# Gated attention with memory and two feed-forward blocks on one core: first-half scores in fp32 from two heads' data in the row halves, mask on TensorE, memory products in row halves

## The chip, the cores and the metric

One core of one Trainium2 chip runs the whole program. The metric is device time in microseconds (us) of one execution; the lower the better. Three executions of the kernel before took 965.35, 965.72 and 968.41 us.

## What is computed

The input has 4 batches (B), 8 heads (H), 576 positions (S) and 64 values per head (D). For each head:

```python
scores = q @ k.T / sqrt(64); causal mask; a = softmax(scores); local = a @ v
q_p = phi(q)                      # phi(x) = where(x > 0, x, exp(x) - 1) + 1
mem = (q_p @ M_prev) / (q_p @ z_prev + 1e-6)
out = g * mem + (1 - g) * local   # g = sigmoid(beta), one number per head
```

The heads of a token side by side are 512 values; the 2304 tokens then go through two feed-forward blocks: `((x @ w1) * (x @ w2)) @ w3 @ w_out` (512 to 1024 to 1024 to 512) and `h = x @ w_in; (h * tanh(softplus(h))) @ w_out` (512 to 2048 to 512). Inputs and output are fp32.

## The kernel before

**Precision.** TensorE multiplies in two ways here. A product of two fp32 tiles is one call in the code and two pairs of weight load and matmul in the trace. Where a faster product is wanted, each operand is split into a rounded part (type fp32r, a cast on ScalarE, ACT) and a remainder (a subtraction on VectorE, DVE, `lo`, line 341 with `sub`, line 333), and two or three fp32r products are added in PSUM.

**Tasks.** A task is a pair of heads (128 partitions: 64 rows of one head, 64 of the other) of one batch. Batch 0 is split by queries: tasks 0 to 3 take positions 0 to 287 (`hfs == (0,)`, the "first halves"), tasks 4 to 7 positions 288 to 575; the tasks of batches 1 to 3 take all 576. Tasks 0 to 11 (`T.f32`, `AVF=12`) multiply values and memory in fp32, the later ones in fp32r.

**One head of a first half** goes through these steps. `load_qk` (465) brings K transposed and Q transposed into a tile `ld`, each twice, in the upper and the lower 64 partitions (128 x 672). `prep` (473) makes from it a tile `QK`: a cast on ACT of all 672 columns (480), the remainder of K in the lower half on DVE (484, 64x384) and the remainder of Q (485, 128x288). With K and its remainder stacked in the 128 rows, two fp32r products per piece give the scores: `SC` (530) issues for each of three pieces (288, 160 and 32 queries wide) two pairs of weight load and matmul into one PSUM bank. Then DVE adds the causal mask to the bank (560): one operation of 128x256 and one of 128x32. The maximum over keys is taken on ACT, DVE and GpSimd (571, 569, 580), `SE` (582) subtracts it and takes the exponential, and `AV` (604) multiplies by the values.

**Once per task**, `phi` (488) loads Q of both heads again into a tile `pl` and makes phi(Q) (`PH`); `MEM` (503) multiplies it by the memory, for each half of 288 queries: `fm`, one fp32 product with the block-diagonal 128x128 matrix of both heads, and `fn`, one with the two columns of z. Two copies on ACT move the results out: 128x288 into `mnl` (526) and 2x288 into rows 0 and 1 of `R` (528). `AV` of the second head ends the task: the norms in `R` go through DRAM and come back spread over the partitions (644 to 661), two DVE operations combine (662, 663), and the result becomes `x`, the input of the feed-forward part.

**Weights.** The feed-forward weights come as pairs of 32-bit words and are converted on the core (`conv`, 673: one operation on ACT, two on DVE; `load_w` adds a cast and a remainder). w3 and w_out of the first block are multiplied with each other first, in 64 fp32 products of 512 columns (`w3_mm`, 718, tiles `wB` and `wD`). This is what TensorE does between the heads of the first halves.

**The order.** Nothing is ordered by the chip's queues at run time alone: every step is recorded as an operation with an engine and a cost (`op`, 82), and `Recorder.schedule` (111) works out, before the program is built, in which order each engine gets them. TensorE takes the operation with the lowest recorded number, feed-forward work counting 300 more (`GB=300`), so attention goes first where it is ready; the other engines take the one with the longest tail behind it. All transfers are on the one queue of SyncE (SP), in that order. Tiles come from rows of buffers (`ld` and `QK` two each, `PH`, `M`, `R` and `pl` one, eight PSUM banks `g`); an operation that needs a buffer waits until all users of its former owner are done. A changed cost therefore changes the order of the whole list.

The second feed-forward block runs after all attention is done, from about 580 us on.

Of the kernel before, what the change touches and what calls it, by code (L numbers as in the profile page):

```python
# [10 lines left out]
BF16 = mybir.dt.bfloat16  # L11
I32 = mybir.dt.int32
AF = mybir.ActivationFunctionType
# [249 lines left out]
def kernel(  # L263
    ctx: ExitStack,
    tc: tile.TileContext,
    qk: bass.AP,
    q: bass.AP,
    v: bass.AP,
    mz: bass.AP,
    beta: bass.AP,  # L270
    moe_w1: bass.AP,
# [76 lines left out]

    mask = const.tile([P, P], BF16, name="mask")
    eps = const.tile([P, 1], F32, name="eps")  # L350
    bt = const.tile([P, NP], F32, name="bt")
# [14 lines left out]

    fb, fg, fm_ = Fixed(bt), Fixed(gsc), Fixed(mask)
    fx2 = [Fixed(x2d) for _ in range(2 * B)]
# [6 lines left out]
    def triangle():  # L375
        idx, low = tri.tile[:, 0], tri.tile[:, 1]
        nc.vector.memset(mask, 0.0)
        for y in range(1, 4):
            nc.vector.memset(mask[32 * y:32 * y + 32, 0:32 * y], NEG)
        nc.vector.memset(idx[:, 0:1], 0.0)  # L380
        for y in range(5):
            nc.vector.tensor_scalar(out=idx[:, 1 << y:2 << y], in0=idx[:, 0:1 << y], scalar1=float(1 << y), scalar2=None, op0=ALU.add)
        nc.vector.transpose(low, idx)
        nc.vector.tensor_tensor(out=low, in0=idx, in1=low, op=ALU.is_lt)
        for y in range(4):
            r = slice(32 * y, 32 * y + 32)
            nc.vector.tensor_scalar(out=mask[r, r], in0=low[r], scalar1=NEG, scalar2=None, op0=ALU.mult)

    op("dve", 1300, triangle, w=[tri, fm_])

# [50 lines left out]
    def load_vm(T):  # L441
        j = T.nj
        n = 2 * j * DV
        if T.f32:
            M = T.M = buf("M", [P, VZ])
            dma(lambda: Vf.tile[:, T.i % 2, 0:j], lambda: v[T.b, T.p, :, 0:j], 512 * n, w=[(Vf, T.i % 2)])
            dma(lambda: M.tile, lambda: mz[T.b, T.p], 66560, w=[M])
            return
        raw = buf("vr", [P, VZ + 2 * NJ * DV])
        mr = lambda: raw.tile[:, 0:VZ]  # L450
        vr = lambda: raw.tile[:, VZ:VZ + n].rearrange("p (j t d) -> p j t d", t=2, d=DV)
        dma(vr, lambda: v[T.b, T.p, :, 0:j], 512 * n, w=[(raw, 0)])
        dma(mr, lambda: mz[T.b, T.p], 66560, w=[(raw, 1)])

        M = T.M = buf("M", [P, 2 * VZ], F32R)
        act(VZ, lambda: M.tile[:, 0:VZ], mr, [(raw, 1)], [(M, 0)])
        for a, b, c in ((0, P, VZ + 2), (P, VZ, VZ)):
            lo(b - a, lambda a=a, b=b, c=c: M.tile[:, c:c + b - a], lambda a=a, b=b: mr()[:, a:b], lambda a=a, b=b: M.tile[:, a:b], [(raw, 1), (M, 0)], [(M, 1)])
        act(n, lambda: Vb.tile[:, 0, 0:j], vr, [(raw, 0)], [(Vb, 0)])
        lo(n, lambda: Vb.tile[:, 1, 0:j], vr, lambda: Vb.tile[:, 0, 0:j], [(raw, 0), (Vb, 0)], [(Vb, 1)])  # L460

    def load_qk(T, t):
        h = 2 * T.p + t
        T.qk = getattr(T, "qk", {})
        d = T.qk[t] = buf("ld", [P, KQ])
        q0 = SK + T.x0
        for y, (a, b) in enumerate({(0,): [(K3, SK + HS)], (1,): [(0, SK), (SK + HS, KQ)], (0, 1): [(0, KQ)]}[T.hfs]):  # L470
            dma(lambda a=a, b=b: d.tile[:, a:b], lambda a=a, b=b: qk[T.b, h, :, a:b], 512 * (b - a), w=[(d, y)])

    def prep(T, t):
        d = T.qk[t]
        T.Q = getattr(T, "Q", {})
# [12 lines left out]
    def phi(T):  # L488
# [5 lines left out]
        ev = lambda: e.tile[:, 0:w]  # L494
        dma(xv, lambda: q[T.b, 2 * T.p:2 * T.p + 2, :, T.x0:T.x0 + w].rearrange("t d s -> (t d) s"), 512 * w, w=[x1])
        act(w, ev, xv, [x1], [e], False, AF.Exp)
        act(w, xv, xv, [x1], [x1], False, AF.Identity, bias=one)
        op("dve", t_dve(w), lambda: nc.vector.scalar_tensor_tensor(out=ev(), in0=ev(), scalar=1.0, in1=xv(), op0=ALU.min, op1=ALU.max), r=[e, x1], w=[e])
# [4 lines left out]
    def MEM(T):  # L503
# [3 lines left out]
        for hf in T.hfs:  # L507
            pm, pn = gbuf(), gbuf()
            qs = T.qs(HS * hf, HS * hf + HS)
            if T.f32:  # L510
                rd, cost, nz = [PH, M], 2 * 248, 2
                fm = lambda pm=pm, qs=qs: mm(pm.tile[:, 0:HS], M.tile[:, 0:P], PH.tile[:, qs], True, True)
                fn = lambda pn=pn, qs=qs: mm(pn.tile[0:2, 0:HS], M.tile[:, P:VZ], PH.tile[:, qs], True, True)
            else:
                rd, cost, nz = [(z, y) for z in (PH, M) for y in range(2)], 3 * t_mm(HS), 4

                def fm(pm=pm, qs=qs):
                    for y, (a, b) in enumerate(HL):
                        mm(pm.tile[:, 0:HS], M.tile[:, (VZ + 2) * a:(VZ + 2) * a + P], PH.tile[:, b, qs], y == 0, y == 2)

                def fn(pn=pn, qs=qs):
                    mm(pn.tile[0:4, 0:HS], M.tile[:, P:VZ + 2], PH.tile[:, 0, qs], True, False)
                    mm(pn.tile[0:4, 0:HS], M.tile[:, P:VZ + 2], PH.tile[:, 1, qs], False, True)

# [5 lines left out]
    def SC(T, t):  # L530
        Q = T.Q[t]
        T.m = m = buf("t", [P, T.w])
        T.s = []
        mkey = []
        for i, pieces in enumerate(T.banks):
            s = gbuf()
            T.s.append(s)

            def f(s=s, pieces=pieces):
                for j, q0, q1, c in pieces:  # L540
                    o = s.tile[:, c:c + q1 - q0]
                    kc = (j * P + K3) % SK
                    for y in range(2):
                        qc = SK + y * S + q0
                        mm(o, Q.tile[:, kc:kc + P], Q.tile[:, qc:qc + q1 - q0], y == 0, y == 1)

            op("pe", sum(2 * t_mm(q1 - q0) for _, q0, q1, _ in pieces), f, r=[(Q, x) for x in T.qkeys], w=[s])
            for i2, cs, m0, m1 in T.masks:
                if i2 != i:
                    continue  # L550
# [53 lines left out]
    def AV(T, t):  # L604
# [38 lines left out]
        rb = buf("Rr", [P, 2, W])  # L643
        dma(lambda: d0.tile[0:2], lambda: R.tile[0:2, :], 9216, r=[(R, (2, hf)) for hf in T.hfs], w=[(d0, 0)])
        dma(lambda: d0.tile[2:4], lambda: R.tile[32:65:32, :], 9216, r=[(R, (x, z)) for x in range(2) for z in range(len(T.outs))], w=[(d0, 1)])
# [349 lines left out]

_INS = ['qk', 'q', 'v', 'mz', 'beta', 'moe_w1', 'moe_w2', 'moe_w3', 'moe_w_out', 'moe2_w_in', 'moe2_w_out']
_OUTS = [((2304, 512), 'float32')]
# [49 lines left out]
```

## Time and profile before

| | |
|---|---|
| median of three executions | 965.72 us (965.35 to 968.41) |
| the profiled execution | 965.84 us |
| its span, first to last instruction | 964.1 us |
| TensorE (PE) busy | 945.7 us, 98% |
| VectorE (DVE) busy | 725.8 us, 75% |
| ScalarE (ACT) busy | 607.0 us, 63% |
| GpSimd (POOL) busy | 86.4 us, 9% |

"PE" is matmuls and "PEld" weight loads, which overlap them. Matmuls are pipelined: one that is shown as 0.6 us long may follow the one before it after 0.4 us, so the distance between two starts is the better measure of what a matmul costs, and a PE that is 98% busy isn't at its peak for all that time. The granted clock of TensorE is 1.00 in all slices of the span.

### The profile page before, as it was taken

What the parts mean: (1) busy time and instruction counts of PE and PEld (TensorE: products, weight loads), DVE (VectorE), ACT (ScalarE), POOL (GpSimd) and SP (SyncE); (2) the same over time, 40 slices, a digit from 0 to 9 for tenths busy, and PEclk for the clock granted to TensorE, in tenths of its full rate; (3) what the DMA queues carried; (4) which work ended last, traced back from release to release, by engine and by line L of the source; (5) the groups of instructions that cost most, each with busy time, mean ns of one, the idle gap of its engine ahead of it and who ended that gap; (6) DMA issues with size and microseconds to landing.
All of it is one profiled execution on the core that took longest, in us unless ns stands there. A gap on an engine that the chain in (4) does not pass through costs nothing.

```text
span 964.1 us, 15222 instructions
## 1 busy us (share of the span) xinstructions
PE 945.7 (98%) x5440; PEld 808.9 (84%) x5440; DVE 725.8 (75%) x1643; ACT 607.0 (63%) x1240; POOL 86.4 (9%) x70
## 2 busy tenths in 40 slices
PE   6999999999999999999999999999999999999998
PEld 3454878778999999999999988888888888998997
DVE  7999999899999989896653987547554756565663
ACT  6677877778797778775433776446444544554653
POOL 1210012322222012120000000000000000000000
PEclk9999999999999999999999999999999999999999
DMA  9689655542433422302641740020002001100000
GB/s 351 215 246 303 201 167 153 156 141 82 142 98 91 151 75 83 107 26 83 203 153 49 228 167 1 1 81 7 1 1 83 1 0 32 46 1 17 34 1 33
DMA packets 48316, 96.62 MB, mean 100 GB/s; under 512 B 11024, under 2 KB 23344, under 8 KB 48240
## 3 DMA queue, kind: packets, MB, share of 16 engines
q1 hardware_dynamic: 48240, 95.64, 31.3%
q8 instruction: 43, 0.70, 0.3%
q14 instruction: 33, 0.27, 0.1%
HBM read 85.85 MB, written 9.77 MB: 99 GB/s over the span
## 4 chain that ended last, share of the span: by engine, by line
PE 67%; DVE 18%; ACT 6%; DMA 4%; issue 3%; SPq 1%; POOL 0%; DVEq 0%; ACTq 0%; POOLq 0%
PE g L330 67%; DVE t L347 4%; DVE QK L333 3%; DMA Rr<-d 2%; DVE e L333 1%; DVE e L347 1%; ACT t L339 1%; DVE mnl L347 1%; DVE g L560 1%; SPq L327 1%; DVE u L333 1%; DVE t L686 1%; ACT mnl L337 1%; DMA wA<-in_moe_w_out_dram 1%; ACT R L337 1%
## 5 line engine op out<-in xcount | busy, mean ns | idle before, releaser
L330 PE MATMUL g<-u,wA 128*128 128x288 f32 (+2 forms) x1008 | 162.6, 314 | 1.0 <-ACT u L337 0.6
L330 PEld LDWEIGHTS g<-u,wA 128*128 128x128 f32 x1008 | 147.2, 188 | 9.9 <-ACT u L337 1.0
L347 DVE TENSOR_TENSOR t<-g,t 128x288 f32<-128x288 f32 (+6 forms) x344 | 121.3, 380 | 22.2 <-PE g L330 14.4
L580 POOL PARTITION_ALL_REDUCE t<-t x64 | 85.8, 1342 | 352.0 <-DVE t L347 282.5
L330 PE MATMUL g<-x,wB 128*128 128x288 f32 x768 | 110.7, 298 | 0.8 <-DVE t L347 0.8
L330 PEld LDWEIGHTS g<-x,wB 128*128 128x128 f32 x768 | 104.7, 188 | 3.3 <-DVE t L347 1.4
L339 ACT ACTIVATE x<-x,two 128x512 f32<-128x512 f32 (+1 forms) x80 | 54.4, 680 | 70.8 <-DVE x L830 70.8
L339 ACT ACTIVATE x<-g 128x512 f32<-128x512 f32 (+1 forms) x98 | 55.0, 561 | 65.2 <-PE g L330 63.9
L330 PE MATMUL g<-e,V 128*65 128x320 f32 (+12 forms) x576 | 90.3, 303 | 1.9 <-ACT e L339 1.5
L833 DVE SCALAR_TENSOR_TENSOR x<-g,x 128x512 f32<-128x512 f32 (+1 forms) x80 | 51.0, 637 | 43.0 <-ACT x L339 42.6
L330 PEld LDWEIGHTS g<-e,V 128*65 128x65 f32 (+1 forms) x576 | 66.2, 136 | 20.3 <-ACT e L339 3.0
L829 DVE TENSOR_SCALAR x<-x 128x512 f32<-128x512 f32 (+1 forms) x80 | 31.8, 397 | 61.8 <-ACT x L339 60.0
L330 PE MATMUL g<-QK 128*128 128x320 f32 (+7 forms) x464 | 72.8, 298 | 5.2 <-DVE QK L333 5.1
L337 ACT CAST x<-x 128x512 fp32r<-128x512 f32 (+1 forms) x80 | 46.1, 577 | 50.4 <-DVE x L347 50.3
L330 PEld LDWEIGHTS g<-QK 128*128 128x128 f32 x464 | 64.0, 193 | 14.8 <-DVE QK L333 7.8
L333 DVE TENSOR_TENSOR t<-x 128x512 fp32r<-128x512 f32 (+1 forms) x80 | 50.9, 637 | 31.9 <-ACT x L337 30.6
L330 PE MATMUL g<-wB,wD 128*128 128x512 f32 x128 | 61.6, 619 | 3.9 <-DVE wD L686 2.1
L333 DVE TENSOR_TENSOR QK<-ld,QK 64x640 fp32r<-64x640 f32 (+1 forms) x80 | 61.7, 772 | 3.5 <-ACT QK L337 1.9
L330 PE MATMUL g<-x,wD 128*128 128x288 f32 x384 | 57.0, 298 | 0.0
L337 ACT COPY t<-g 128x288 f32<-128x288 f32 (+2 forms) x96 | 36.5, 394 | 32.5 <-PE g L330 24.7
L330 PE MATMUL g<-x,wE 128*128 128x288 f32 x384 | 56.2, 300 | 0.5 <-DVE e L347 0.4
L347 DVE TENSOR_TENSOR x<-x 128x512 f32<-128x512 f32 (+1 forms) x80 | 51.0, 637 | 6.0
(147 smaller groups left out, 1815.6 us busy)
## 6 DMA issues: line engine op xcount, KB each, us to landing
ld<-in_qk_dram SPq DMA_DIRECT2D x24, 608.0 KB
u<-in_moe_w_dram SPq DMA_DIRECT2D x26, 512.0 KB
Rr<-d SPq DMA_DIRECT2D x24, 288.0 KB
mnl<-in_moe_w_out_dram SPq DMA_DIRECT2D x11, 512.0 KB
mnl<-in_moe_w_in_dram SPq DMA_DIRECT2D x11, 512.0 KB
x2d<-t SPq DMA_DIRECT2D x16, 288.0 KB
out_dram<-x SPq DMA_DIRECT2D x18, 256.0 KB
wA<-in_moe_w_out_dram SPq DMA_DIRECT2D x8, 512.0 KB
```

Source lines behind the costliest of these rows:

```text
L327: op("sp", max(500, nbytes / 340.0), lambda: nc.sync.dma_start(out=dst(), in_=src()), r, w)
L330: nc.tensor.matmul(out=o, lhsT=lhsT, rhs=rhs, start=start, stop=stop)
L333: eng.tensor_tensor(out=o, in0=a, in1=b, op=ALU.subtract)
L337: op("act", t_act(n, psum), lambda: nc.scalar.copy(out=o(), in_=i()), r, w)
L339: op("act", t_act(n, psum), lambda: nc.scalar.activation(out=o(), in_=i(), func=func, **kw), r, w)
L347: op(eng, t_dve(n) if eng == "dve" else t_pool(n), lambda: e.tensor_tensor(out=o(), in0=a(), in1=b(), op=alu), r, w)
L560: nc.vector.tensor_tensor(out=o, in0=o, in1=mv, op=ALU.add)
L580: op("pool", 430 + 2.6 * (b - a), lambda mv=mv: nc.gpsimd.partition_all_reduce(mv(), mv(), P, bass_isa.ReduceOp.max), r=[(m, x)], w=[(m, x)])
L686: op("dve", t_dve(512), lambda: nc.vector.scalar_tensor_tensor(out=ci(), in0=ci(), scalar=3, in1=lw(), op0=ALU.logical_shift_left, op1=ALU ...
L829: op("dve", t_dve(n, True), lambda: nc.vector.tensor_scalar(out=w_(), in0=u(), scalar1=E20, scalar2=2.0, op0=ALU.min, op1=ALU.add), r=[ub_ ...
L833: op("dve", t_dve(n), lambda: nc.vector.scalar_tensor_tensor(out=u(), in0=hv(), scalar=2.0 ** -8, in1=u(), op0=ALU.mult, op1=ALU.mult), r= ...
```

## The change

It changes the four tasks of first halves and the memory products of tasks 0 to 11.

- First halves: K (a new input `kp`, without Q) and Q of both heads are loaded once per task, one head in each 64 rows, 128x384 and 128x288. `prep` does nothing for them. `SC` of the first head issues the scores of both heads as one operation: for each of the three pieces one fp32 product with the upper 64 rows into one bank, one with the lower 64 rows into another, and then the mask, as a product of a bf16 unit matrix and the bf16 mask, added in PSUM to each of the two banks. The DVE operations of line 560 are left out for tasks 0 to 3 (`PEM=4`). `phi` reads Q from the same tile and loads nothing.
- Memory products of tasks 0 to 11: a new input `mp` has for each head 64 rows of 128 columns: the 64 columns of its memory, and one column of z that stands in the other head's half. Each half of 288 queries takes one fp32 product with the upper 64 rows and one with the lower 64 rows, into two banks, in one operation. Four copies on ACT move the results out: 64x288 twice into `mnl`, 1x288 twice into rows 0 and 96 of `R`.

```diff
     MIX=5,
     AVF=12,
+    PEM=4,
     W3G=1,
...
+        nc.vector.memset(unit, 0.0)
+        for y in range(4):
+            r = slice(32 * y, 32 * y + 32)
+            nc.vector.tensor_tensor(out=unit[r, r], in0=idx[r], in1=low[r], op=ALU.is_equal)
...
+            self.raw = hfs == (0,)
...
-            M = T.M = buf("M", [P, VZ])
+            M = T.M = buf("M", [P, P])
             dma(lambda: Vf.tile[:, T.i % 2, 0:j], lambda: v[T.b, T.p, :, 0:j], 512 * n, w=[(Vf, T.i % 2)])
-            dma(lambda: M.tile, lambda: mz[T.b, T.p], 66560, w=[M])
+            dma(lambda: M.tile, lambda: mp[T.b, T.p], 65536, w=[M])
...
+        if T.raw:
+            if t == 0:
+                T.kq = buf("ld", [P, KQ])
+                dma(lambda: T.kq.tile[:, K3:SK], lambda: kp[T.b, h:h + 2, :, K3:SK].rearrange("t d s -> (t d) s"), 512 * (SK - K3), w=[(T.kq, 0)])
+                dma(lambda: T.kq.tile[:, SK:SK + T.w], lambda: q[T.b, h:h + 2, :, T.x0:T.x0 + T.w].rearrange("t d s -> (t d) s"), 512 * T.w, w=[(T.kq, 1)])
+            return
...
+        if T.raw:
+            return
...
-        dma(xv, lambda: q[T.b, 2 * T.p:2 * T.p + 2, :, T.x0:T.x0 + w].rearrange("t d s -> (t d) s"), 512 * w, w=[x1])
-        act(w, ev, xv, [x1], [e], False, AF.Exp)
-        act(w, xv, xv, [x1], [x1], False, AF.Identity, bias=one)
+        xi, xr = xv, x1
+        if T.raw:
+            xi, xr = lambda: T.kq.tile[:, SK:SK + w], (T.kq, 1)
+        else:
+            dma(xv, lambda: q[T.b, 2 * T.p:2 * T.p + 2, :, T.x0:T.x0 + w].rearrange("t d s -> (t d) s"), 512 * w, w=[x1])
+        act(w, ev, xi, [xr], [e], False, AF.Exp)
+        act(w, xv, xi, [xr], [x1], False, AF.Identity, bias=one)
...
-                rd, cost, nz = [PH, M], 2 * 248, 2
-                fm = lambda pm=pm, qs=qs: mm(pm.tile[:, 0:HS], M.tile[:, 0:P], PH.tile[:, qs], True, True)
-                fn = lambda pn=pn, qs=qs: mm(pn.tile[0:2, 0:HS], M.tile[:, P:VZ], PH.tile[:, qs], True, True)
...
+
+                def fp(ss=(pm, pn), qs=qs):
+                    for s, r in zip(ss, HALF):
+                        mm(s.tile[:, 0:HS], M.tile[r], PH.tile[r, qs], True, True)
+
+                op("pe", 2 * 248, fp, r=[PH, M], w=[pm, pn])
+                for t, ps in enumerate((pm, pn)):
+                    act(HS, lambda qs=qs, r=HALF[t]: mnl.tile[r, 0, qs], lambda ps=ps, r=HALF[t]: ps.tile[r, 0:HS], [ps], [(mnl, (0, t, hf))], True)
+                    act(HS, lambda qs=qs, r=96 * t: R.tile[r:r + 1, qs], lambda ps=ps, r=64 - 64 * t: ps.tile[r:r + 1, 0:HS], [ps], [(R, (2, t, hf))], True)
+                continue
...
     def SC(T, t):
-        Q = T.Q[t]
...
-            s = gbuf()
-            T.s.append(s)
-
-            def f(s=s, pieces=pieces):
+
+            low = {c: (m0, m1) for i2, cs, m0, m1 in T.masks for c in cs if i2 == i and T.i < CFG["PEM"]}
+
+            def fr(ss, pieces=pieces, low=low):
+
+                for j, q0, q1, c in pieces:
+                    kc, qc = (j * P + K3) % SK, SK + q0 - T.x0
+                    for s, r in zip(ss, HALF):
+                        mm(s.tile[:, c:c + q1 - q0], T.kq.tile[r, kc:kc + P], T.kq.tile[r, qc:qc + q1 - q0], True, c not in low)
+                    for s in ss:
+                        if c in low:
+                            m0, m1 = low[c]
+                            mm(s.tile[:, c:c + m1 - m0], unit, mask[:, m0:m1], False, True)
+
+            def f(s=None, pieces=pieces, low=low):
+                Q = T.Q[t]
...
-                        mm(o, Q.tile[:, kc:kc + P], Q.tile[:, qc:qc + q1 - q0], y == 0, y == 1)
...
-            op("pe", sum(2 * t_mm(q1 - q0) for _, q0, q1, _ in pieces), f, r=[(Q, x) for x in T.qkeys], w=[s])
+                        mm(o, Q.tile[:, kc:kc + P], Q.tile[:, qc:qc + q1 - q0], y == 0, y == 1 and c not in low)
...
+            if T.raw:
+                if t == 0:
+                    T.pair = [gbuf(), gbuf()]
+                    op("pe", sum(2 * max(0.84 * (q1 - q0), 107) + 75 for _, q0, q1, _ in pieces), lambda fr=fr, ss=T.pair: fr(ss),
+                       r=[(T.kq, 0), (T.kq, 1), fm_, fu], w=T.pair)
+                s = T.pair[t]
+            else:
+                s = gbuf()
+                op("pe", 75 * len(low) + sum(2 * t_mm(q1 - q0) for _, q0, q1, _ in pieces), lambda f=f, s=s: f(s),
+                   r=[(T.Q[t], x) for x in T.qkeys] + [fm_, fu] * (len(low) > 0), w=[s])
+            T.s.append(s)
...
-                if i2 != i:
+                if i2 != i or T.i < CFG["PEM"]:
...
-        dma(lambda: d0.tile[0:2], lambda: R.tile[0:2, :], 9216, r=[(R, (2, hf)) for hf in T.hfs], w=[(d0, 0)])
+        if T.f32:
+            dma(lambda: d0.tile[0:2], lambda: R.tile[0:97:96, :], 9216, r=[(R, (2, x, hf)) for x in range(2) for hf in T.hfs], w=[(d0, 0)])
+        else:
+            dma(lambda: d0.tile[0:2], lambda: R.tile[0:2, :], 9216, r=[(R, (2, hf)) for hf in T.hfs], w=[(d0, 0)])
...
+    lay["kp"] = _np.concatenate([k[..., 3 * P_:], k[..., :3 * P_]], axis=-1)
...
+    m = _np.zeros((b, h // 2, 2, d, 2 * d), inputs["M_prev"].dtype)
+    for t in range(2):
+        m[:, :, t, :, t * d:(t + 1) * d] = inputs["M_prev"][:, t::2]
+        m[:, :, t, :, (1 - t) * d] = inputs["z_prev"][:, t::2]
+    lay["mp"] = m.reshape(b, h // 2, 2 * d, 2 * d)
```

## Rows read from the trace of the kernel before

**Rows 1.** Busy time by stretch: stretch, length, engines (instructions), clock, DMA share, GB/s

```profile
0.00:30.00 30.00, 20.26 (x62) 10.09 (x63) 24.65 (x74) 18.64 (x34) 4.74 (x9) 1.00 0.90 338
30.00:57.00 27.00, 26.77 (x98) 13.92 (x97) 24.57 (x69) 17.24 (x37) 5.39 (x4) 1.00 0.71 223
57.00:100.00 43.00, 42.80 (x149) 22.94 (x148) 41.72 (x98) 32.52 (x68) 4.11 (x3) 1.00 0.87 273
100.00:160.00 60.00, 59.13 (x386) 49.23 (x385) 58.00 (x159) 44.74 (x101) 11.12 (x8) 1.00 0.54 170
160.00:220.00 60.00, 58.79 (x367) 46.62 (x367) 55.51 (x154) 48.65 (x113) 16.27 (x13) 1.00 0.47 141
...
400.00:500.00 100.00, 99.77 (x766) 98.78 (x764) 70.54 (x166) 56.28 (x130) 8.12 (x6) 1.00 0.39 118
```

**Rows 2.** Chain of waits, 0 to 57 us: shares by engine and line

```profile
by line: PE g L330 12.2%; issue 12.2%; DMA wA<-in_moe_w_out_dram 10.6%; DVE wD L686 8.8%; DVE QK L333 7.9%; DVE e L347 6.4%; DVE wB L686 6.0%; ACT wB L339 3.7%; DVE wA L684 3.3%; SPq L327 2.9%; DVE t L347 2.7%; DVE wE L684 2.4%; POOL t L580
```

**Rows 3.** Timeline, 0 to 31 us: start, duration, instruction

```profile
3.70 0.75 ACT L337 CAST QK<-ld 128x672 fp32r<-128x672 f32 x1 [1.70 <-DMA ld<-in_qk_dram]
...
5.09 1.77 PE L330 MATMUL g<-QK 128*128 128x288 f32 x6 [5.09 <-DVE QK L333]
...
8.98 1.52 PE L330 MATMUL g<-QK 128*128 128x288 f32 x6
...
12.14 4.52 PE L330 MATMUL g<-wB,wD 128*128 128x512 f32 x6 [1.64 <-DVE wD L686]
```

**Rows 4.** Groups by form, 0 to 57 us: busy, mean ns, idle before

```profile
L337 ACT CAST QK<-ld 128x672 fp32r<-128x672 f32 x8 | 6.0, 750 | 3.0 <-DMA ld<-in_qk_dram 3.0
...
L333 DVE TENSOR_TENSOR QK<-ld,QK 64x384 fp32r<-64x384 f32 x8 | 5.3, 662 | 0.8 <-ACT QK L337 0.4
...
L333 DVE TENSOR_TENSOR QK<-ld,QK 128x288 fp32r<-128x288 f32 x8 | 4.0, 502 | 0.2
...
L560 DVE TENSOR_TENSOR g<-g,mask 128x256 f32<-128x256 f32 x8 | 3.4, 426 | 1.2 <-PE g L330 1.2
...
L560 DVE TENSOR_TENSOR g<-g,mask 128x32 f32<-128x32 f32 x7 | 1.4, 194 | 0.1
```

**Rows 5.** Busy time of the instructions of tile QK alone, first 30 us

```profile
0.00:30.00 30.00, 5.03 (x24) 4.44 (x24) 4.06 (x8) 2.99 (x4) 1.00 0.90 338
```

**Rows 6.** Busy time of line 560 (mask) alone, first 30 us

```profile
0.00:30.00 30.00, 2.06 (x7) 1.00 0.90 338
```

**Rows 7.** DMA issues: tile, queue, count, KB each

```profile
ld<-in_qk_dram SPq DMA_DIRECT2D x8, 336.0 KB
...
pl<-in_q_dram SPq DMA_DIRECT2D x8, 144.0 KB
```

**Rows 8.** Timeline of PE, 36 to 42 us

```profile
38.63 1.23 PE L330 MATMUL g<-PH,M 128*128 128x288 f32 x4
39.78 0.89 PE L330 MATMUL g<-QK 128*128 128x288 f32 x6
40.52 1.96 PE L330 MATMUL g<-wB,wD 128*128 128x512 f32 x4
```

**Rows 9.** Timeline of PE, 170 to 178 us

```profile
172.05 3.43 PE L330 MATMUL g<-u,wA 128*128 128x288 f32 x24
175.32 0.65 PE L330 MATMUL g<-PH,M 128*128 128x288 f32 x2
```

**Rows 10.** Busy time of the instructions that write or read PH

```profile
30.00:100.00 70.00, 3.75 (x12) 1.37 (x12) 1.35 (x3) 1.77 (x4) 1.00 0.81 254
100.00:220.00 120.00, 13.90 (x44) 4.60 (x44) 5.37 (x8) 4.27 (x7) 1.00 0.51 156
```

**Rows 11.** Groups by form, whole span

```profile
L330 PE MATMUL g<-u,wA 128*128 128x288 f32 x768 | 109.1, 297 | 1.0 <-ACT u L337 0.6 <-DVE u L333 0.3
...
L337 ACT COPY mnl<-g 64x288 f32<-64x288 f32 x16 | 6.3, 392 | 1.5 <-PE g L330 1.3
L337 ACT COPY R<-g 1x288 f32<-1x288 f32 x16 | 6.3, 391 | 4.6 <-PE g L330 4.3
```

More of the change, by code (lines that the diff above doesn't have):

```diff
@@ L267 @@
     q: bass.AP,
+    kp: bass.AP,
     v: bass.AP,
     mz: bass.AP,
+    mp: bass.AP,
     beta: bass.AP,
@@ L349 @@
     mask = const.tile([P, P], BF16, name="mask")
+    unit = const.tile([P, P], BF16, name="unit")
     eps = const.tile([P, 1], F32, name="eps")
@@ L365 @@
     nc.vector.memset(eps[64:128], 1e-9)
-    fb, fg, fm_ = Fixed(bt), Fixed(gsc), Fixed(mask)
+    fb, fg, fm_, fu = Fixed(bt), Fixed(gsc), Fixed(mask), Fixed(unit)
     fx2 = [Fixed(x2d) for _ in range(2 * B)]
@@ L387, in triangle @@
             nc.vector.tensor_scalar(out=mask[r, r], in0=low[r], scalar1=NEG, scalar2=None, op0=ALU.mult)
-    op("dve", 1300, triangle, w=[tri, fm_])
+    op("dve", 1300, triangle, w=[tri, fm_, fu])
     X = {}
@@ L510, in MEM, with fm, fn @@
             if T.f32:
-                rd, cost, nz = [PH, M], 2 * 248, 2
-                fm = lambda pm=pm, qs=qs: mm(pm.tile[:, 0:HS], M.tile[:, 0:P], PH.tile[:, qs], True, True)
-                fn = lambda pn=pn, qs=qs: mm(pn.tile[0:2, 0:HS], M.tile[:, P:VZ], PH.tile[:, qs], True, True)
[L514 to L523, printed above, removed]
+                def fp(ss=(pm, pn), qs=qs):
[6 more added lines that the diff above has]
+                continue
+            rd, cost, nz = [(z, y) for z in (PH, M) for y in range(2)], 3 * t_mm(HS), 4
+            def fm(pm=pm, qs=qs):
+                for y, (a, b) in enumerate(HL):
+                    mm(pm.tile[:, 0:HS], M.tile[:, (VZ + 2) * a:(VZ + 2) * a + P], PH.tile[:, b, qs], y == 0, y == 2)
+            def fn(pn=pn, qs=qs):
+                mm(pn.tile[0:4, 0:HS], M.tile[:, P:VZ + 2], PH.tile[:, 0, qs], True, False)
+                mm(pn.tile[0:4, 0:HS], M.tile[:, P:VZ + 2], PH.tile[:, 1, qs], False, True)
             op("pe", cost, fm, r=rd, w=[pm])
@@ L544, in f @@
                         qc = SK + y * S + q0
-                        mm(o, Q.tile[:, kc:kc + P], Q.tile[:, qc:qc + q1 - q0], y == 0, y == 1)
-            op("pe", sum(2 * t_mm(q1 - q0) for _, q0, q1, _ in pieces), f, r=[(Q, x) for x in T.qkeys], w=[s])
+                        mm(o, Q.tile[:, kc:kc + P], Q.tile[:, qc:qc + q1 - q0], y == 0, y == 1 and c not in low)
+                    if c in low:
+                        m0, m1 = low[c]
+                        mm(s.tile[:, c:c + m1 - m0], unit, mask[:, m0:m1], False, True)
+            if T.raw:
[9 more added lines that the diff above has]
+            T.s.append(s)
             for i2, cs, m0, m1 in T.masks:
-                if i2 != i:
+                if i2 != i or T.i < CFG["PEM"]:
                     continue
@@ L993 @@
     rec.flush()
-_INS = ['qk', 'q', 'v', 'mz', 'beta', 'moe_w1', 'moe_w2', 'moe_w3', 'moe_w_out', 'moe2_w_in', 'moe2_w_out']
+_INS = ['qk', 'q', 'kp', 'v', 'mz', 'mp', 'beta', 'moe_w1', 'moe_w2', 'moe_w3', 'moe_w_out', 'moe2_w_in', 'moe2_w_out']
 _OUTS = [((2304, 512), 'float32')]
@@ L1014 @@
     k = _np.pad(inputs["k"].transpose(0, 1, 3, 2), ((0, 0), (0, 0), (0, 0), (0, nj * P_ - s)))
-    k = _np.concatenate([k[..., 3 * P_:], k[..., :3 * P_], lay["q"]], axis=-1)
+    lay["kp"] = _np.concatenate([k[..., 3 * P_:], k[..., :3 * P_]], axis=-1)
+    k = _np.concatenate([lay["kp"], lay["q"]], axis=-1)
     lay["qk"] = _np.concatenate([k, k], axis=2)
```

## The prediction

> **What bounds the kernel now.** First the busy time by stretch. From 400 us on TensorE runs 766 matmuls per 100 us and nothing else is near full: that part follows whatever comes before it, so what is won earlier is kept only as far as TensorE's list moves up. Before that I read four stretches [rows 1]. From 0 to 30 us TensorE does 62 matmuls where the next 27 us hold 98 of about the same mix; at 98 / 27 = 3.63 per us the 62 are 17.1 us of work, so 12.9 us are waiting. DVE is busy 24.65 of these 30 us and the DMA engines 0.90 of them at 338 GB/s. From 30 to 100 us TensorE is dense (26.77 of 27 and 42.80 of 43 us) on the weight products; DVE's idle time has become small too (41.72 of 43 us from 57 us on). From 100 to 160 us DVE is the full one (58.00 of 60 us), and from 160 to 220 us DVE (55.51) and ACT (48.65) share the load while TensorE is shown busy but runs 6.1 to 6.4 matmuls per us instead of 7.66, in part because fp32 ones are longer.
>
> Second the chain of waits to 57 us: no engine owns it. TensorE and issue have 12.2% each, the transfer of `wA` 10.6%, DVE's conversion of `wD` and `wB` 8.8% and 6.0%, `prep` on DVE 7.9% [rows 2]. Third the first steps in time: the data of the first head is there at 3.70, its scores begin at 5.09 only after cast and remainders, the second head's at 8.98, and the weight products begin at 12.14 behind DVE's `wD` [rows 3]. So the start is paced by transfers and DVE's queue together, then TensorE, then DVE.
>
> **Prices on DVE and DMA, and the start.** The change removes 8 remainders of K at 662 ns (5.3 us), 8 of Q at 502 (4.0), 8 wide masks at 426 (3.4) and 8 narrow ones at 194 (1.6): 14.3 us of DVE, all before about 60 us [rows 4]. On ACT it removes 8 casts, 6.0 us [rows 4]. Of DVE's part 4.06 us (`QK`) and 2.06 us (line 560) lie in the first 30 us [rows 5, 6]; against it stand five new operations for the unit matrix, each at most the narrow mask's 194 ns, so 1.0 us: 5.1 us net. They stand in front of the first scores, which now need no cast and no remainder (1.4 us from 3.70 to 5.09) but a second transfer; that start I leave at 5 us, and only the second head gains, 4 us, on an engine that then waits for weights anyway.
>
> Transfers: per task two of 336 KB and one of 144 KB go, 192 + 144 KB come, and on SP's queue three issues become two [rows 7]. The weights queue behind these. Before 30 us six loads of `ld` and three of `pl` are issued, 2448 KB; three tasks now need 1008 KB. The 1440 KB less (1.47 MB) are 4.4 us at 338 GB/s [rows 1]. Both DVE (5.1) and DMA (4.4) must give way for the weight products to come earlier, so the start is worth the smaller, **-4.5 us**. Bounds: nothing, if conversions on ACT or the chain's issue gaps pace it; -8 if the weights also skip waits for each other (12.9 us are there).
>
> **Prices on TensorE.** Four passes of 512 fp32 columns are shown 1.96 us long; less the 0.16 us by which a last matmul outlasts its turn (below) that is 0.45 per pass, 0.88 ns per column. A memory product of four passes takes 1.15 us start to start (38.63 to 39.78) and a head's six score passes 0.74 (39.78 to 40.52) [rows 8]. The 16 memory products are thus 18.4 us, two heads' scores 1.48.
>
> After the change a pass of 288 columns costs 0.253 us, one of 160 0.141, one of 32 about a sixth of 0.74, 0.123. No product of 64 rows stands in the trace, so whether the two halves run beside each other is bounded from both sides. In series, as every pair of passes in rows 8 does, a memory product is 4 x 0.253 = 1.01 (16 x -0.14 = -2.2 us), and a pair of heads 4 x (0.253 + 0.141 + 0.123) = 2.07 plus six mask products at 0.123, 0.74, together 2.81 (+1.33 x 4 = +5.3 us). Side by side, a memory product is 0.51 to 0.76 (the second half starts one pass late), say 0.60 (16 x -0.55 = -8.8 us), and a pair 1.03 + 0.74 = 1.77 (+0.29 x 4 = +1.2 us). I take side by side: the halves have different rows, different banks and no operand in common, so nothing in the program makes one wait for the other. The Trainium skill, "TensorE: Matmul & The Clock Gate", section "The mechanism" of its Part 3, has products in different row groups start about 4 ns apart; by it the terms would be the -8.8 and +1.2 above, by the rows in series -2.2 and +5.3, and no row of the trace before shows which.
>
> What of it counts: of the memory products' passes 12 lie in 30 to 100 us and 44 in 100 to 220 us [rows 10], three and eleven products of four; the other two stand in the start, where TensorE waits anyway. The three in the dense stretch count whole (-1.65), the eleven, where TensorE waits now and then, half (-3.0), the scores half (+0.6): **-4 us**. In series the same weights give -0.4, -0.8 and +2.7, so +1.5 us.
>
> **What is left of DVE.** 14.3 - 6.1 = 8.2 us of DVE go from the stretch 30 to 60 us, where TensorE is dense and can use none of it. DVE reaches 100 us that much earlier, TensorE only by the two terms above; of the 3.5 us or so between them I give the stretch that DVE fills **-1.5 us** (bounds 0 and -3.5).
>
> **ACT.** Per memory product two copies become four, each some 0.39 us whatever its rows (64x288 takes 392 ns, 1x288 391) [rows 11]: +0.78 us, 16 times, +12.5 us, less the casts' 6.0. Eleven of them fall in 100 to 220 us, +8.6 us, where ACT is busy 44.74 + 48.65 of 120 us [rows 1]. Behind them in ACT's queue wait the exponentials and casts of the running head, and two banks instead of one stay taken. I price it **+1 us** (bounds 0 and the 8.6 us).
>
> **Sum:** -4.5 - 4 - 1.5 + 1 = -9; the profiled execution took 965.84, its span 964.1; so 956.8, about 957. It stands 0.12 us over the median of the three. This measurement tells about 0.3% from no change, 2.9 us: faster is below 962.9, slower above 968.7.
>
> **Rivals.**
> A. *TensorE empties at each change of row layout.* The row for 288-column products shows 297 ns where their distance, 24 in 172.05 to 175.32, is 136: 0.16 us of tail that the next normally covers [rows 9, 11]. Each pair changes between 64 and 128 rows six times (masks between pieces), each memory product twice: 24 + 32 = 56 times 0.16, 9.0 us, of which about half counts by the weights above, 4.5. 961. For it: the change alternates layouts more than needed. The Trainium skill, "TensorEngine Tiling (Array Packing)", section "Key Properties", says a change of tiling mode drains the engine; no row here shows such a change. 0.14.
> B. *The halves run in series.* TensorE's term goes from -4 to +1.5: 962. For it: rows 8 show only that. 0.09.
> C. *Slower: half-row products don't cover their weight loads.* Every pass on the same rows would wait for its own load, 4.44 us / 24 = 0.185 [rows 5]. A memory product is then 4 x (0.253 + 0.185) = 1.75 (+0.60) and a pair 12 passes, 2.07 + 12 x 0.185, plus six masks at 0.31, 6.2 (+4.7). At the same weights: 1.8 + 3.3 + 9.4 = +14.5, with the other terms -5, so 975. It decides from the point where a 288-column pass takes over 0.29 us, a quarter of 1.15. Against it: full-row fp32 passes do cover theirs. 0.07.
> D. *What is won early is waited away.* The stretch 57 to 100 us has DMA at 0.87 and weights on the same queue; if these pace the attention of the later heads, only half of TensorE's term and the cost on ACT remain, -1: 965. 0.13.
>
> **How the numbers follow.** The forecast has 0.57, its own range 949 to 962. The range 947 to 965 takes in A, B, D and the better bound of the start (-8); C and the tails stay out. Faster: 0.56 of the forecast, 0.11 of A, 0.05 of B, 0.05 of D, 0.77. Same: 0.01, 0.03, 0.04, 0.07, 0.15. Slower: C and a rest of D, 0.08.
>
> **What would show it.** Right: weight products begin before 9 us and the first 30 us hold over 75 matmuls; DVE's total falls by 13 to 14 us, ACT's rises by 6 to 7; in the trace the lower half's first pass overlaps the upper half's second, and a memory product takes 0.5 to 0.76 us start to start; the granted clock stays at 1.00. A shows as gaps of some 0.16 us around each pair, B as 1.0 us per memory product, C as distances of 0.4 us per pass, D as an unchanged time at which the first feed-forward products begin and more idle time of TensorE from 100 us on. The prediction is wrong if the end moves by less than 3 us with the start moved by 4, or if the list of operations comes out in another order with a new wait of several us.

## The result, and the profile after

The changed kernel takes 977.58 us (median of 5 runs, 976.59 to 978.36) where the kernel before takes 965.72 (965.35 to 968.41): ratio 1.0118 [1.0104, 1.0132], **slower by 11.4 us** by this ratio, where 9 us faster (957) was forecast. The profiled execution took 977.28 us, its span is 975.5. All ratios below are to the kernel before on the same chip, with their 95% interval; 0.1% is about 1 us.

The totals (the page's first part, busy time of each engine) moved the way that was forecast, but not as far on VectorE and further on ScalarE: VectorE 716.8 (-9.0, forecast -13 to -14), ScalarE 616.1 (+9.1, forecast +6 to +7), TensorE 947.8 (+2.1).

```profile
PE 947.8 (97%) x5464; PEld 808.3 (83%) x5464; DVE 716.8 (73%) x1616; ACT 616.1 (63%) x1264; POOL 85.9 (9%) x70
```

Busy time by stretch of the changed kernel, as in [rows 1] (columns: stretch, length, engines with their instructions, granted clock, DMA share, GB/s):

```profile
0.00:30.00 30.00, 20.01 (x68) 9.40 (x70) 18.81 (x64) 15.23 (x30) 6.14 (x10) 0.94 0.79 297
30.00:57.00 27.00, 25.17 (x106) 11.76 (x102) 17.43 (x50) 17.13 (x38) 5.51 (x4) 1.00 0.60 193
57.00:100.00 43.00, 41.28 (x125) 20.37 (x125) 40.26 (x95) 33.42 (x68) 2.87 (x2) 1.00 0.79 262
100.00:160.00 60.00, 58.72 (x385) 49.58 (x386) 58.26 (x156) 46.33 (x104) 10.23 (x8) 1.00 0.55 165
160.00:220.00 60.00, 56.31 (x355) 45.07 (x353) 51.05 (x136) 51.56 (x114) 13.90 (x12) 1.00 0.48 140
220.00:400.00 180.00, 174.59 (x1318) 166.22 (x1318) 166.99 (x428) 144.56 (x334) 37.32 (x28) 1.00 0.34 103
400.00:500.00 100.00, 99.79 (x766) 98.53 (x765) 75.13 (x175) 60.37 (x138) 9.97 (x7) 1.00 0.39 118
```

From 0 to 57 us VectorE has 13 us less to do than before and the DMA engines stand idle more, and yet TensorE gains nothing (the higher counts are the masks' products): the room is there and goes unused. From 57 us on TensorE loses: 125 matmuls for 149, then (after 385 for 386) 355 for 367. From 220 to 400 us, where of the changed products only one falls (at 223.45, slipped in from before), the same row of the kernel before has 1360 matmuls against 1318:

```profile
220.00:400.00 180.00, 177.89 (x1360) 171.65 (x1359) 168.58 (x425) 145.30 (x330) 36.68 (x27) 1.00 0.36 108
```

After 400 us the two are alike (766 and 766). The first use of `u,wA` slips from 143.8 to 152.7 us, 9 of the 11 us.

Why the start does not come earlier is in the timeline (start, duration, instruction, idle time before it and its releaser). TensorE:

```profile
3.66 1.33 PE L333 MATMUL g<-ld 64*128 64x288 f32 x4 [3.66 <-DMA ld<-in_q_dram]
...
12.56 1.92 PE L333 MATMUL g<-e,V 128*65 128x288 f32 x6 [4.04 <-ACT e L342]
...
14.29 2.06 PE L333 MATMUL g<-wB,wD 128*128 128x512 f32 x2
```

and SP's queue, which issues the loads:

```profile
19.63 2.47 SPq L330 DMA_DIRECT2D d<-R  x2
30.51 0.34 SPq L330 DMA_DIRECT2D M<-in_mp_dram  x1
...
31.37 0.42 SPq L330 DMA_DIRECT2D wE<-in_moe_w_dram  x1
31.84 0.43 SPq L330 DMA_DIRECT2D u<-in_moe_w_dram  x1
```

The scores begin 1.4 us earlier (3.66 for 5.09, [rows 3]), but the list now has the first head's product with V ahead of the first weight product, so TensorE stands 4.0 us for ScalarE and begins on the weights at 14.29 instead of 12.14. Without that product it couldn't have begun before 13.0 either: VectorE converts the first `wD` from 12.31 to 13.01 (it was done at 12.09 before). SP stands from 22.1 to 30.5 us at the load of `M`: its one buffer is free only after the second task's memory product (29.68 below), and two weight loads wait behind it.

The row halves themselves (TensorE's timeline):

```profile
29.68 0.76 PE L333 MATMUL g<-PH,M 64*128 64x288 f32 x4
30.37 1.06 PE L333 MATMUL g<-e,V 128*65 128x288 f32 x6
...
35.27 0.76 PE L333 MATMUL g<-ld 64*128 64x288 f32 x4
35.96 0.29 PE L333 MATMUL g<-mask,unit 128*128 128x128 bf16 x2
36.18 0.54 PE L333 MATMUL g<-ld 64*128 64x160 f32 x4
36.65 0.28 PE L333 MATMUL g<-mask,unit 128*128 128x128 bf16 x2
36.87 0.41 PE L333 MATMUL g<-ld 64*128 64x32 f32 x4
37.21 0.21 PE L333 MATMUL g<-mask,unit 128*128 128x32 bf16 x2
37.28 1.96 PE L333 MATMUL g<-wB,wD 128*128 128x512 f32 x4
```

A memory product's four passes take 30.37 - 29.68 = 0.69 us (1.15 in [rows 8]); in series they would be 1.01. The halves run side by side. A pair of heads takes 37.28 - 35.27 = 2.01 us, of which its masks 0.22 + 0.22 + 0.07. These are prices from 29 us on; the first two pairs, before 20 us, take 3.52 and 2.93 us, as the kernel before, too, had its first products slower (2.28 us for the first memory product).

### The profile page after: what moved, and what is told of

Read it like the earlier page. It is cut to its first block, busy times and chain, and to the rows that moved or that the text cites. A ratio compares the mean times of both kernels' runs of the same rounds, so it can differ in the third digit from the quotient of the medians.

```text
span 975.5 us, 15275 instructions
## 1 busy us (share of the span) xinstructions
PE 947.8 (97%) x5464; PEld 808.3 (83%) x5464; DVE 716.8 (73%) x1616; ACT 616.1 (63%) x1264; POOL 85.9 (9%) x70
## 4 chain that ended last, share of the span: by engine, by line
PE 71%; DVE 16%; ACT 6%; DMA 3%; issue 3%; SPq 0%; POOL 0%; DVEq 0%; ACTq 0%
PE g L333 71%; DVE t L350 4%; DVE QK L336 3%; DMA Rr<-d 2%; DVE mnl L350 2%; DVE e L336 1%; DVE e L350 1%; ACT mnl L340 1%; ACT e L342 1%; ACT QK L340 1%; DVE g L613 1%; ACT R L340 1%; DVE u L336 1%; DMA u<-in_moe_w_dram 1%; ACT t L342 1%
## 5 line engine op out<-in xcount | busy, mean ns | idle before, releaser
L350 DVE TENSOR_TENSOR t<-g,t 128x320 f32<-128x320 f32 (+6 forms) x344 | 120.5, 382 | 25.6 <-PE g L333 12.4
L333 PE MATMUL g<-QK 128*128 128x64 f32 (+3 forms) x416 | 64.4, 295 | 0.6 <-DVE QK L336 0.3
L333 PEld LDWEIGHTS g<-QK 128*128 128x128 f32 x416 | 56.9, 190 | 5.1 <-DVE QK L336 0.8
L333 PEld LDWEIGHTS g<-x,wE 128*128 128x128 f32 x384 | 52.2, 189 | 3.9 <-DVE e L350 1.8
```

The source lines that it names most:

```text
L333: nc.tensor.matmul(out=o, lhsT=lhsT, rhs=rhs, start=start, stop=stop)
L350: op(eng, t_dve(n) if eng == "dve" else t_pool(n), lambda: e.tensor_tensor(out=o(), in0=a(), in1=b(), op=alu), r, w)
```

## The experiments

**First the parts apart.** Scores alone (the memory products put back):

```diff
-            M = T.M = buf("M", [P, P])
+            M = T.M = buf("M", [P, VZ])
...
-                op("pe", 2 * 248, fp, r=[PH, M], w=[pm, pn])
+                rd, cost, nz = [PH, M], 2 * 248, 2
```

> The changed kernel with the memory products of the kernel before (one 128-row product for both heads, one for z, two copies each); only the first halves are new. Theory copies (the doubled ScalarE copies of the memory products cost the time): without them the first halves alone are a gain, 956 to 962 us. Theory queue (SyncE's queue stands still behind loads of the one buffer M, which waits for a memory product that TensorE's list now has late, and the weights stand behind it): still slow, 972 us or more. Theory list (every change of costs and lengths makes another list of operations, and this list fits the chip badly in the first 57 us): anything from 960 to 978.

Measured 974.31, 1.0062 [1.0038, 1.0086]. Memory products alone (the mirror edit on the kernel before):

> The kernel before with the new memory products alone (row halves, four copies); scores, masks and loads as before. Theory copies: slower than before by 5 us or more, 971 us and up, with ScalarE's busy time up by some 12 us. Theory queue: within 3 us of before, since the loads of the start are unchanged. Theory list: anything from 960 to 978. TensorE's own saving, 0.4 us each, 16 times, would speak for 960.

975.83, 1.0077 [1.0048, 1.0107]; TensorE waits 4.7 us in nine pieces for ScalarE's copies into `mnl`. The whole change with the masks left to VectorE (`PEM=4` to `PEM=0`):

> The changed kernel with the mask of the first four tasks added by VectorE as before, none by TensorE. VectorE gets some 5 us back, TensorE loses about 3 us and the changes between 64 and 128 rows within a pair of scores. A theory that the row changes cost (rival A of the prediction): faster than the changed kernel by 2 us or more. Theory queue or copies: within 2 us of 977.6. Theory list: a difference of several us either way.

970.95, 1.0041 [1.0026, 1.0056]. And the load that holds SP, moved to the unused columns of the tile with K and Q:

```diff
+        if T.raw:
...
+            dma(lambda: T.kq.tile[:, 0:P], lambda: mp[T.b, T.p], 65536, w=[(T.kq, 2)])
+            return
```

> The changed kernel, but the memory matrix of the first four tasks is loaded into unused columns of the tile that holds their K and Q, so that its load doesn't wait for the memory product of the task before. Theory queue: SyncE no longer stands from 22 to 30 us, the weights come earlier and the time falls by 4 us or more, to 973.5 or less. Theory copies: within 2 us of 977.6. Theory list: a difference of several us either way, without the stretch 22 to 30 us having become denser.

973.78, 1.0066 [1.0043, 1.0090]: by the ratios 5.0 of the 11.4 us come back. The profiled execution was one of the slow ones of its five (975.88; they run from 972.18 to 976.06). In it SP no longer stands at the load of `M` (issued at 22.20), and yet the first 57 us hold 172 matmuls for the changed kernel's 174, and `u,wA` starts at 153.6. So either part alone costs, and their costs do not add. SP's stop may be a part of the loss, at most these 5 us; where they come from isn't shown. The first three edits also make the planner write another list; the fourth hardly does in the first 57 us.

**Then the list.** The order of the kernel before imposed on the changed work (`RANK`, one place per operation; one that still lacks an input or a buffer lets the next go first), for the whole change and for the memory products alone:

```diff
-        for o in self.schedule():
+        todo = sorted(ops, key=lambda o: RANK[o.idx])
```

> The changed kernel, all of its work, but each engine gets its operations in the order of the kernel before: the order is written into the kernel as a list of ranks, the new operations stand where their counterparts stood. Theory list (the loss comes from the new order that the planner works out, not from the new operations): faster than the changed kernel by 10 us or more and not slower than the kernel before, 955 to 967 us. Theory copies (ScalarE's added 12 us cost the time): still 972 us or more. Theory queue (loads of M hold the weights): in between, since the old order of loads puts weights first.

> The kernel before with the new memory products alone, in the order of the kernel before. Its own plan took 975.8. Theory list: 958 to 967, the same as before or a little faster. Theory copies: 972 or more, as with its own plan.

988.64, 1.0227 [1.0210, 1.0244], and 986.66, 1.0210 [1.0192, 1.0229]: the old places are the slowest of all lists tried for the new work. And the kernel before with nothing altered but one constant of the planner, so that the same instructions stand in other places:

```diff
-                rd, cost, nz = [PH, M], 2 * 248, 2
+                rd, cost, nz = [PH, M], 2 * 250, 2
```

> The kernel before, with one number of the planner changed: the cost that it assumes for the old memory products is 500 ns instead of 496. Not one instruction is another, only their order. Theory list: the time moves by 2 us or more, most likely up. Theories copies and queue say nothing of it; if the order doesn't matter, 967 within 1.5 us.

```diff
-    SPM=300,
+    SPM=310,
```

> The kernel before, with another number of the planner changed: the delay that it assumes ahead of a transfer, 310 ns instead of 300. Again only the order differs. Theory list: the time moves by 2 us or more, most likely up to between 968 and 980. If the order doesn't matter, 967 within 1.5 us.

The first: 967.39, 1.0006 [0.9996, 1.0015]. The second: 978.53, **1.0124 [1.0109, 1.0139]**. The order alone can cost as much as the whole change, and in the same place (its row of stretches):

```profile
220.00:400.00 180.00, 169.90 (x1284) 162.04 (x1283) 152.90 (x385) 134.16 (x302) 32.38 (x26) 1.00 0.34 96
```

**Other lists of the changed work** (masks on VectorE; the lines shown are of the first, the expectations name the constants of the others). The constants, here and below, were picked by replaying lists with the durations of the traces, each engine in its order; what counts is what the chip took.

```diff
-    GB=300,
+    GB=320,
...
-    RES=2,
+    RES=1,
```

> The change with the masks of the first four tasks back on VectorE (as in the run of that name, 971 us) and with four of the planner's own constants moved (GB 300 to 320, SPM 300 to 320, MIX 5 to 7, RES 2 to 1), which alter only where instructions stand in the queues. Theory 1, the new list costs the time: another list of the same work lands elsewhere, by more than 5 us from 971, and a good one below the kernel before; 958 to 966. Theory 2, the work itself costs the time (ScalarE's doubled copies, TensorE's half-row passes): whatever the list, it stays within 4 us of 971.

> As the list before it, with other constants: GB 320, RES 1, DMM 800 to 1200, and ScalarE's copies from PSUM priced 59 ns dearer in the plan (their recorded 390 ns is above the plan's 291). Theory 1: 958 to 966. Theory 2: 967 to 975.

> As the two lists before it, with GB 350 and the last rate at which feed-forward work is mixed in 3.7 for 3.6. Theory 1: 958 to 966, and the three lists differ among each other by several us. Theory 2: 967 to 975, the three within 2 us.

967.76, 966.00 and 970.43: 1.0012 [0.9996, 1.0028], 0.9988 [0.9975, 1.0002], 1.0037 [1.0022, 1.0052]. With the run with `PEM=0` they span 5 us for one and the same work; none is clearly below the kernel before, and none reaches 957.

**The copies by themselves**, the list of the kernel before untouched:

```diff
-            op("act", t_act(n, psum), lambda: nc.scalar.copy(out=o(), in_=i()), r, w)
+            op("act", t_act(n, psum), lambda: [nc.scalar.copy(out=o(), in_=i()) for _ in range(times)], r, w)
```

> The kernel before, its list untouched, with each of the 32 copies of the memory products of the first 12 tasks done twice by ScalarE (32 more copies at 0.39 us, 12.5 us of ScalarE). It prices the copies alone. Theory 2: they stand on the path between 100 and 280 us, where ScalarE and VectorE share the load, and the time rises by 8 to 12 us to 975 to 979. Theory 1 (the cost was priced right at about 1 us): 967 to 969.

974.54, 1.0080 [1.0062, 1.0098]: 7.7 of the 12.5 us of added copies arrive at the end. Its stretch where ScalarE and VectorE share the load has 18 matmuls less than [rows 1]:

```profile
160.00:220.00 60.00, 56.93 (x349) 44.25 (x347) 53.18 (x144) 49.78 (x114) 15.19 (x12) 1.00 0.51 148
```

**What each part is worth in a list that suits it.** Scores alone with masks on VectorE, in two lists, and then the first list held with the masks on TensorE:

```diff
-    PEM=4,
+    PEM=0,
...
-    GB=300,
+    GB=270,
```

> Only the scores' part of the change (fp32 scores from data as loaded), masks on VectorE and memory products as before, with another list: the planner's GB 300 to 270 and RES 2 to 3. Theory 1 (new list) and theory 2 (the memory products' doubled copies cost 8 us) together: with the copies gone and a list that suits it, the start's 4 us and VectorE's 9 us come out, 957 to 963, below the kernel before. Theory 3, no part of the change is worth anything on the chip: 967 or more in any list.

> The same work in a second list (GB 320, RES 1), to see what of the first one's time is the list's luck. Theories 1 and 2: 958 to 966, within 4 us of the first. Theory 3: 967 or more.

> The first of these two lists held, instruction by instruction (ScalarE's and SP's queues unchanged), with the masks of the four tasks on TensorE instead of VectorE: 24 mask products in, 16 mask operations of VectorE (5 us) out. In the changed kernel's trace the six masks of a pair take 0.49 us of TensorE and the changes between row layouts some 0.1 us each, so 3 to 4 us of TensorE for four pairs, about half of it before 31 us where TensorE waits anyway. Theory 1 (masks on TensorE cost only through the list): within 2 us of the first list. Rival: the mask products stand on TensorE's path: 3 to 5 us slower.

964.12, **0.9971 [0.9959, 0.9983]**; 966.36, 0.9996 [0.9982, 1.0010]; 967.57, 1.0003 [0.9991, 1.0015]. The scores' part gains about 3 us, and TensorE's masks take it back: +0.32% with the list held.

Then halves only for the memory products of the first six tasks:

```diff
+        T.half = T.f32 and T.i < CFG["MH"]
...
-                op("pe", 2 * 248, fp, r=[PH, M], w=[pm, pn])
+                op("pe", 620, fp, r=[PH, M], w=[pm, pn])
```

> The scores' part with masks on VectorE, and the memory products in the rows' halves for the first six tasks only, those before about 110 us, where ScalarE has room; a list of its own (GB 320, RES 1, and the plan's prices of the pair, the memory product and PSUM copies nearer to the recorded ones). Theory 2: without the copies in 110 to 220 us the halves cost nothing and TensorE's 0.4 us each is kept: 956 to 962, as the first list or up to 3 us faster. Rival: the merged product waits for two PSUM banks and ScalarE's copies wherever it stands: 3 to 6 us slower than the first list.

962.27, **0.9954 [0.9940, 0.9968]**: faster than both kernels. That list held, with no halves, and with halves for all sixteen products:

> The list of the run with halves for six tasks (962 us) held, and its six memory products in halves put back to the two full-row products and two copies of the kernel before, at the same places in the queues. What the halves are worth where ScalarE has room: theory 2 (TensorE's 0.4 us each are kept, the copies cost little): 963 to 966. Rival (the merged product waits for two banks and four copies wherever it stands): 958 to 961.

> The same list held, with the other ten memory products of the first 12 tasks, those from about 110 us on, in halves too: 20 more copies of ScalarE (7.8 us), ten merged products, TensorE's part 4 us shorter. Theory 2 (copies cost where ScalarE and VectorE share the load): 967 to 972. Rival (the copies cost nothing of themselves, it was the list): 959 to 964.

964.44, 0.9970 [0.9956, 0.9984], and 975.06, **1.0070 [1.0051, 1.0090]**. The six early products in halves give about 1.5 us, which is not clear of noise (the intervals overlap). With the ten late ones the same list is 11.2 us slower by the ratios. Not all of that is theirs: the last of the early products, up to which TensorE does the same work in both, starts 2.2 us later in the profiled execution with all, whose granted clock was 0.66 from 10 to 20 us. First the run with six, then the run with all (the clock is the third number from the end):

```profile
10.00:20.00 10.00, 9.06 (x32) 4.63 (x32) 8.24 (x23) 6.60 (x15) 1.49 (x2) 1.00 1.03 410
101.48 0.76 PE L334 MATMUL g<-PH,M 64*128 64x288 f32 x4
```

```profile
10.00:20.00 10.00, 9.32 (x31) 5.20 (x32) 7.54 (x20) 5.80 (x13) 1.64 (x2) 0.66 1.03 409
103.66 0.76 PE L569 MATMUL g<-PH,M 64*128 64x288 f32 x4
```

So some 9 to 11 us go with the ten late products in this list. The stretches of the run with six:

```profile
160.00:220.00 60.00, 60.00 (x381) 48.20 (x379) 56.48 (x153) 50.36 (x115) 15.99 (x12) 1.00 0.47 136
220.00:400.00 180.00, 177.10 (x1361) 171.36 (x1360) 166.05 (x416) 143.22 (x326) 32.49 (x26) 1.00 0.36 104
```

and of the run with all:

```profile
160.00:220.00 60.00, 56.16 (x336) 45.48 (x334) 48.08 (x128) 48.20 (x106) 16.46 (x12) 0.94 0.45 120
220.00:400.00 180.00, 176.39 (x1339) 168.56 (x1338) 165.31 (x421) 145.75 (x335) 35.57 (x28) 1.00 0.36 104
```

45 matmuls are missing between 160 and 220 us, with VectorE and ScalarE less busy too: everything waits in turn. How, shows its timeline:

```profile
176.31 0.76 DVE L586 TENSOR_TENSOR mnl<-mnl,Rr 128x576 f32<-128x576 f32 x1 [3.12 <-DMA Rr<-d]
176.48 0.75 PE L569 MATMUL g<-PH,M 64*128 64x288 f32 x2
...
177.68 0.43 ACT L576 CAST x<-mnl 128x288 fp32r<-128x288 f32 x1 [2.02 <-DVE mnl L586]
...
178.51 0.36 ACT L576 COPY mnl<-g 64x256 f32<-64x256 f32 x1
178.92 0.75 PE L569 MATMUL g<-PH,M 64*128 64x288 f32 x2 [1.70 <-ACT mnl L576]
...
179.60 0.67 PE L569 MATMUL g<-u,wA 128*128 128x288 f32 x3
```

The first half starts at 176.48, the second at 178.92: its bank is free only when ScalarE has copied an attention product out of it (178.51). The halves no longer run side by side, and the product takes 3.1 us to the next one's start. ScalarE was not busy all that time: a cast of `x` ahead of this copy in its queue stood 2.02 us for VectorE, which had stood 3.12 us for the transfer of the norms (0.60 at the same place of the run with six). So this tear is a wait handed on from queue to queue; that the added copies set it off isn't shown. In all, TensorE waits 5.1 us for copies into `mnl` between 100 and 280 us in this run, 0.3 in the one with six; 2.1 of the 5.1 stand ahead of memory products, and `mnl` takes copies of attention products too (waits of TensorE: us in total, times, longest; in that order):

```profile
PE g L569 <- ACT mnl L576: 5.1, 7, 1.7
```

```profile
PE g L334 <- ACT mnl L341: 0.3, 1, 0.3
```

The full-row product at the same place of the run with six takes 1.15 us, and TensorE does not wait:

```profile
170.23 1.22 PE L334 MATMUL g<-PH,M 128*128 128x288 f32 x4
171.38 1.06 PE L334 MATMUL g<-u,wA 128*128 128x288 f32 x6
```

## Why the prediction was wrong

**Start, -4.5.** VectorE's and the transfers' relief came (18.81 for 24.65 us, DMA 0.79 for 0.90); the gain did not: the weight products began at 14.29 us and the first 30 us hold 68 matmuls, where the signs of being right were before 9 us and over 75. The step took the queues' order as given and only shortened what stands in them. Its own lower bound, conversions on ScalarE that pace the start, is one of the things that VectorE now meets: up to 57 us it waits 5.4 us for ScalarE's part of `wD` and `wB` (the changed kernel, then the kernel before; us in total, times, longest):

```profile
DVE wD L742 <- ACT wD L342: 2.9, 4, 0.8
DVE wB L742 <- ACT wB L342: 2.5, 3, 1.6
```

```profile
DVE wB L686 <- ACT wB L339: 1.0, 3, 0.5
```

In a list that suits the work, the weight products of the run with six run from 10.5 to 93.5 us (12.1 to 95.2 before, 14.3 to 101.2 in the changed kernel), so some 1.7 us are there:

```profile
L334 PE MATMUL g<-wB,wD x128: 591/592/1222, 10.5 to 93.5; 128*128 128x512 f32 x128
```

**TensorE, -4.** Side by side was right. The Trainium skill, "TensorE: Matmul & The Clock Gate", section "The mechanism" of Part 3, has products in different row groups start almost together; the trace agrees, 0.69 us for four passes, where one half alone took 0.68 (178.92 to 179.60 above). The size was off by a price of the change between 64 and 128 rows. A product's two pairs of passes are 2 x 0.253 = 0.51 by the forecast, and two changes add 0.18; the 160-column piece (36.18 to 36.65) has 0.47 for 0.28, again 0.19 more. It goes with the change and not with the pass: where no masks stand between the pieces, the same twelve passes follow each other in 1.10 us (run with six, first two lines), where the changed kernel's pair without its masks is 2.01 - 0.51 = 1.50 with four changes more; and two memory products in a row are shown 1.24 us long (run with all, third line), where one is shown 0.76: the second adds 0.48, little less than its 0.51.

```profile
30.22 1.17 PE L334 MATMUL g<-ld 64*128 64x288 f32 x12
31.32 1.06 PE L334 MATMUL g<-e,V 128*65 128x288 f32 x6
```

```profile
197.57 1.24 PE L569 MATMUL g<-PH,M 64*128 64x288 f32 x8
```

That is some 0.09 us per change, rival A's price at little more than half its 0.16. A product is 0.09 dearer than forecast (16 times, 1.4 us), a pair 0.24 (4 times, 1.0 us). The pair's masks were counted half. With their changes of layout they are 2.01 - 1.10 = 0.91 us of a pair, 3.6 in all; with the list held they cost 3.1 us, though VectorE loses 5 us of work.

**ScalarE, +1: the step that failed.** The copies were seen and counted (+12.5 us, 8.6 of them between 100 and 220), and then priced at the low end of 0 to 8.6. Doubling them alone measured 7.7. What the sentence named beside them, "two banks instead of one stay taken", was not priced: in a held list the ten late products cost some 9 to 11 us though TensorE's part of them is 4 to 5 us shorter, and TensorE's waits for copies into `mnl` rose from 0.3 to 5.1 us. ScalarE's share (44.74 + 48.65 of 120 us, [rows 1]) looked like room. It was not: in the run with all, ScalarE and VectorE are both less busy from 160 to 220 us (48.20 and 48.08 for 50.36 and 56.48), so that time went in waits and not in work.

**The list: no term at all.** The prediction's last sentence names a list in another order with a new wait of several us as what would make it wrong, but the sum had no price for it. The chip's price for an order is from 0.06% to 1.24% with no instruction changed. By the parts, each with a list held or of its own: scores -2.8, masks +3.1, early halves -1.5, late halves +11.2 (some 2 of it the clock of the start), together +10.0 of the 11.4 measured. This sum is no proof: the lists differ, and in list b the same late halves leave the whole at 0.9988 of the kernel before, 3.3 us above the run with six. How the changed kernel's 11.4 us divide between its list and its late halves therefore stays open; that each of them can be that large is shown. The changed kernel with TensorE's masks in other lists was not tried.

Rival A was right in mechanism and too dear: at 0.09 us its 56 changes are about 5 us of TensorE's time instead of 9.0, an estimate from the rows above, and not what made the kernel slower by 11.4. B's series did not show, nor did C's passes that each wait for a weight load: by C the twelve passes of a pair without masks would take 2.07 + 12 x 0.185 = 4.29 us, and they take 1.10. D, won early and waited away, is nearest: the start's room was not used, but the loss came from copies and order rather than from the weights' transfers.

## What to carry to other kernels

Where a planner writes the queues, a change of durations is a change of order: before pricing parts, measure what the order alone is worth by moving a constant that changes no instruction, and give the range at least that width. When a product is split so that it fills two banks, count the instructions that empty them, on the engine that does it, in the stretch where it happens; the version that won, by 0.46%, splits six of the sixteen products, early ones, and 0.30% of that is there without any split. A held list is the tool to price one part: it separated about 1.5 us of gain, not clear of noise, from some 9 to 11 of loss in the same edit. Count changes of row layout too: the same twelve passes took 1.10 us in a row and 1.50 in three pieces.

## What was not expected of the hardware

TensorE's granted clock, 1.00 in all slices of the profiled execution before, fell for short stretches in others. In the changed kernel TensorE was busy 2.95 of 5 us, and then ran at 0.66 over the next 5, so partly at the lower level of 1.2 GHz: 8 matmuls in 4.76 us (stretches of the changed kernel).

```profile
20.00:25.00 5.00, 2.95 (x11) 1.29 (x9) 4.53 (x13) 3.10 (x7) 3.03 (x2) 1.00 1.04 404
25.00:30.00 5.00, 4.76 (x8) 1.96 (x10) 3.27 (x7) 1.89 (x4) 0.00 (x0) 0.66 0.01 5
```

In the run with all halves the same follows the waits of 170 to 180 us: 40 matmuls in 10 us where the next 10 hold 67.

```profile
170.00:180.00 10.00, 8.30 (x48) 5.88 (x47) 6.82 (x20) 6.96 (x16) 1.38 (x2) 1.00 0.43 127
180.00:190.00 10.00, 9.81 (x40) 7.20 (x39) 7.17 (x23) 8.06 (x19) 3.18 (x3) 0.66 0.36 100
190.00:200.00 10.00, 9.69 (x67) 7.90 (x66) 9.56 (x28) 9.04 (x20) 3.44 (x3) 1.00 0.46 116
```

Waiting alone does not decide it. The kernel before waited in its first 30 us too and kept 1.00; and the runs with six and with all, which do the same work in the same order there and wait 3.6 and 3.8 us ahead of their first weight product, show 1.00 and 0.66 from 10 to 20 us. That pair also gives a price: the second memory product starts at 25.24 in the one and at 27.18 in the other, 1.9 us later. What the clock depends on stays open.
